# A new order of all engines for a one-core kernel of block attention and a gated MLP: fillers on TensorE, some VN on ScalarE, moved tiles

## The chip, the cores and the metric

One NeuronCore of a Trainium2 chip runs the whole program. The metric is the time of one execution on the device in microseconds (us). The engines are TensorE (PE; its weight loads are listed as PEld), VectorE (DVE), ScalarE (ACT), GpSimd (POOL) and SyncE (SP), which here only issues DMAs.

## What is computed

Inputs: q, k, v of 4 batches x 8 heads x 768 positions x 64, a decay lam per head, and the weights of a gated MLP. First comes linear attention with decay in blocks of 64, then the MLP with a mixing of positions:

```
for b in range(nb):                                    # blocks of 64 positions
    intra = (qb @ kb.T) * Dmask ; intra = intra @ vb   # inside the block
    inter = (qb * lam_pow) @ kv_state
    out[:, :, sl] = intra + inter
    kv_state = lam_block * kv_state + (kb * rev_pow).T @ vb
h = maximum(x @ w_in, 0)                               # x: heads side by side, 4 x 768 x 512
u, v = h[..., :512], h[..., 512:]
v_n = (v - mean(v)) / sqrt(var(v) + 1e-06)             # over the 512
v_s = einsum('ts,bsd->btd', w_spatial, v_n) + b_spatial[None, :, None]
out = (u * v_s) @ w_out                                # 4 x 768 x 512, float32
```

## The kernel before

The 4 x 768 positions are worked through in 12 steps n of 256 positions, three to a batch. The decay is folded into k and q by powers of lam counted from the middle of the sequence, so that scores need only a 0/1 mask and the state is only added to. All order is written out by hand: ORDER (from L16) is a list of tokens, each naming a step, its indices and, last, the engine (T TensorE, D VectorE, A ScalarE, P GpSimd, S SyncE). Each engine executes its tokens strictly in the order of the list; semaphores between engines follow from the tiles that are read and written. The last numbers of a token on TensorE and of the copies behind it are PSUM banks; bank 7 holds the running state.

The steps, by token:

- LK, LQ, LV load k, q, v of step n (512 KB each) into one of three buffers each; SP issues them, and the load of n waits until the buffer's last reader (KM or QM or QC, VC of n-3) is done.
- WI, WS, WO load the weights through GpSimd's queue with a cast to bf16, BS the bias through SP.
- LB, LN, LL, LX: powers of lam (Ln, a product, Exp). LT (L221) makes a second table of powers for q along the free dimension, from positions made by pos (L201).
- KM and QM (L287, both print as L289): k or q times its power, cast to bf16, half a step per token (kc, qc; two buffers each). QC (L282): q cast without the power. VC: v cast to bf16 (vb).
- TK and TQ: transposes of kc and qc on TensorE into PSUM; EK and EQ bring them to kT and qT, EQ (L332) multiplied by LT's table. From step 5 on DK and DQ do the transposes by DMA from SP instead, straight to kT and qT.
- SC: scores, MK (L354): mask and cast. KV: state update, SS: copy of the state. AV: attention output, in an inter part (L388) and an intra part (L397). FN: one-element copy that releases it. EX: copy to xT.
- PV (L422), PU (L460): x times the v and u half of w_in; EV and EU apply the relu.
- BN, RA, RD: mean and variance, square root, reciprocal. VN (L449 to L452): normalised v, on VectorE.
- WT, EW: transposes of w_spatial. GP puts the bias into PSUM, PW (L486) multiplies by w_spatial over all six 128-row tiles of a batch, GM multiplies by u. So PW of a batch needs every VN of that batch.
- PO (L497), EO, ST: product with w_out, copy, store. PH, EH, SH do one tile of the last batch in two halves.
- GT (L242): a one-element copy on GpSimd that holds a weight load back until an input has landed. `one` fills a tile of ones; FL (L265) would run matmuls on it whose result nobody reads, but no FL token is in this list.

In the old list PW of batch 0 begins after attention of steps 0 to 2 and the PV and PU of these; attention of step 3 comes between its PW tokens.

Of the kernel before, what the change touches and what calls it, by code (L numbers as in the profile page):

```python
# [16 lines left out]
one.D lam.A LK.0.S msk.P mkc.D LB.0.T LN.0.A posk.P LL.D LX.A KM.0.0.D pos.P idn.P TK.0.0.1.T KM.0.1.P  # L17
TK.0.1.2.T LQ.0.S QC.0.1.D TQ.0.1.3.T LT.0.A QC.0.0.P TQ.0.0.4.T EQ.0.0.4.D LT.1.A EQ.0.1.3.D LK.1.S KM.1.1.P
TK.1.1.5.T EK.0.0.1.A SC.0.0.3.4.T EK.0.1.2.A LQ.1.S QC.1.0.P EK.1.1.5.A GT.1.1.P WI.0.P KM.1.0.D LV.0.S
SC.0.1.0.1.T LV.1.S TK.1.0.6.T EK.1.0.6.A TQ.1.0.2.T LQ.2.S LK.2.S QC.1.1.P TQ.1.1.5.T MK.0.0.3.4.D EQ.1.0.2.D  # L20
MK.0.1.0.1.D VC.0.A KV.0.0.T AV.0.0.3.6.T SS.0.0.A FN.0.3.6.A LV.2.S QC.2.1.P BS.S LK.3.S GT.1.2.P WI.1.P
EQ.1.1.5.D SC.1.1.0.1.T SC.1.0.4.5.T MK.1.0.4.5.D KV.0.1.T SS.0.1.A KM.2.0.P GT.2.1.P WS.0.P LQ.3.S LT.2.A
AV.0.1.3.6.T LV.3.S LK.4.S VC.1.D KV.1.0.T LQ.4.S SS.1.0.A KV.1.1.T KM.2.1.P LK.5.S MK.1.1.0.1.D AV.1.0.2.4.T
QC.2.0.A TQ.2.1.5.T EX.0.1.6.D WS.1.P TQ.2.0.0.T EQ.2.0.0.D LQ.5.S VC.2.P FN.1.2.4.A AV.1.1.2.4.T LV.4.S
EX.1.0.2.D EQ.2.1.5.D EX.1.1.4.A PV.1.0.1.T EX.0.0.3.D SS.1.1.D PV.0.1.6.T EV.0.1.6.A PV.1.1.0.T EV.1.1.0.A
KM.3.0.P KM.3.1.P QC.3.2.P GT.2.2.P WO.P EV.1.0.1.D BN.1.0.D BN.0.1.D TK.2.0.2.T BN.1.1.D PV.0.0.5.T VC.3.P
TK.2.1.4.T EK.2.1.4.D EK.2.0.2.A SC.2.0.0.1.T MK.2.0.0.1.D SC.2.1.3.4.T MK.2.1.3.4.D EV.0.0.5.A RA.1.A BN.0.0.D
RA.0.A RD.1.D LV.5.S RD.0.D PU.1.0.6.T PU.1.1.2.T KV.2.0.T SS.2.0.A EU.1.0.6.A AV.2.0.0.1.T FN.2.0.1.D VN.0.0.D
VN.0.1.D PU.0.1.3.T EU.0.1.3.A KM.4.0.P AV.2.1.0.1.T EX.2.0.0.A EX.2.1.1.D GP.0.0.0.4.A EU.1.1.2.A GP.0.0.1.5.A
PU.0.0.6.T VN.1.1.D VN.1.0.D EU.0.0.6.D PV.2.0.3.T KM.4.1.P EV.2.0.3.A BN.2.0.D PV.2.1.0.T EV.2.1.0.A BN.2.1.D  # L30
WT.0.0.1.T WT.1.0.2.T EW.1.0.2.A EW.0.0.1.D RA.2.A RD.2.D VN.2.0.D WT.2.0.6.T EW.2.0.6.D PU.2.0.3.T GP.0.2.0.0.A
PU.2.1.2.T VN.2.1.D PW.0.0.0.4.T EU.2.0.3.A EU.2.1.2.A WT.1.1.1.T EW.1.1.1.A WT.2.1.6.T EW.2.1.6.A GP.0.3.0.3.D
GM.0.0.0.4.D GP.0.1.1.2.A PW.0.2.0.0.T GM.0.2.0.0.D GP.0.1.0.4.A WT.0.1.1.T EW.0.1.1.D PW.0.3.0.3.T TK.3.2.6.T
EK.3.2.6.A TQ.3.2.0.T PW.0.1.0.4.T GM.0.1.0.4.D EQ.3.2.0.D PW.0.1.1.2.T GM.0.1.1.2.D GM.0.3.0.3.D PW.0.0.1.5.T
GM.0.0.1.5.D KV.3.0.T SC.3.0.0.1.T MK.3.0.0.1.D SC.3.1.2.3.T MK.3.1.2.3.D GP.0.2.1.4.A PW.0.2.1.4.T TK.4.2.6.T
QC.4.2.A TQ.4.2.5.T EQ.4.2.5.D GM.0.2.1.4.D GP.0.3.1.0.A PW.0.3.1.0.T AV.3.0.1.2.T FN.3.1.2.D SS.3.0.A KV.3.1.T
KM.5.1.P EK.4.2.6.A SC.4.0.3.4.T GM.0.3.1.0.D KM.5.0.D DK.5.S AV.3.1.1.2.T EX.3.1.2.A EX.3.0.1.A SC.4.1.5.6.T
MK.4.1.5.6.D PO.0.2.0.T EO.0.2.0.A PO.0.4.2.T EO.0.4.2.D QM.5.1.P QM.5.0.D DQ.5.S VC.5.P PO.0.3.1.T PU.3.0.5.T
PV.3.1.6.T PV.3.0.0.T VC.4.A SS.3.1.D KV.4.0.T MK.4.0.3.4.D AV.4.0.2.3.T EV.3.0.0.D BN.3.0.D PO.0.5.4.T
EU.3.0.5.A SS.4.0.A KV.4.1.T EV.3.1.6.A BN.3.1.D LK.6.S KM.6.0.P FN.4.2.3.A AV.4.1.2.3.T EX.4.1.3.D SS.4.1.A  # L40
LV.6.S EX.4.0.2.A RA.3.A RD.3.D PO.0.1.0.T EO.0.1.0.A EO.0.3.1.A KV.5.0.T SC.5.0.5.6.T MK.5.0.5.6.D SC.5.1.2.3.T
MK.5.1.2.3.D SS.5.0.A PO.0.0.0.T EO.0.0.0.A LQ.6.S QM.6.0.P PV.4.1.1.T PV.4.0.5.T LK.7.S KM.7.0.P LQ.7.S
KM.6.1.D VN.3.0.D LQ.8.S DK.6.S EO.0.5.4.A AV.5.0.2.6.T FN.5.2.6.D PU.4.0.3.T EV.4.1.1.A EV.4.0.5.A QM.6.1.P
AV.5.1.2.6.T BN.4.0.D VC.6.A KV.6.0.T GP.1.2.0.0.D EX.5.0.2.D PU.4.1.4.T EU.4.0.3.A EX.5.1.6.A EU.4.1.4.A
VN.3.1.D BN.4.1.D PV.5.1.1.T EV.5.1.1.D RA.4.A RD.4.D BN.5.1.D PV.5.0.5.T LV.7.S EV.5.0.5.A BN.5.0.D RA.5.A
VN.4.1.D VN.4.0.D RD.5.D VN.5.0.D PU.3.1.2.T EU.3.1.2.A DQ.6.S QM.8.1.P QM.8.0.P VN.5.1.D KM.7.1.D DK.7.S
PU.5.0.3.T PU.5.1.6.T QM.7.1.D QM.7.0.D DQ.7.S PW.1.2.0.0.T EU.5.0.3.D SS.6.0.A GM.1.2.0.0.D LK.8.S LK.9.S
LV.8.S GP.1.3.1.4.A PW.1.3.1.4.T GP.1.0.0.1.A EU.5.1.6.A PW.1.0.0.1.T GM.1.3.1.4.D GM.1.0.0.1.D GP.1.0.1.5.A
PW.1.0.1.5.T GM.1.0.1.5.D GP.1.1.1.2.A PW.1.1.1.2.T SC.6.0.3.4.T MK.6.0.3.4.D SC.6.1.0.1.T MK.6.1.0.1.D
GP.1.2.1.6.A VC.7.A GP.1.3.0.5.A KV.6.1.T PW.1.3.0.5.T GM.1.3.0.5.D KM.8.1.P KM.8.0.P PW.1.2.1.6.T GP.1.1.0.3.A  # L50
SS.6.1.A PW.1.1.0.3.T GM.1.1.1.2.D GM.1.2.1.6.D AV.6.0.0.4.T FN.6.0.4.D KV.7.0.T SS.7.0.A SC.7.1.1.2.T
GM.1.1.0.3.D AV.6.1.0.4.T EX.6.1.4.A DQ.8.S SC.7.0.5.6.T DK.8.S KV.7.1.T PO.1.4.3.T EX.6.0.0.D PU.6.0.4.T
# [33 lines left out]
def kernel(  # L86
# [84 lines left out]
    def bank(b):  # L171
        return ps[:, b]
# [387 lines left out]
```

## Time and profile before

| | us |
|---|---|
| median of 3 runs | 153.12 (152.53 to 153.46) |
| span of the profiled execution, first to last instruction | 151.8 |
| TensorE busy in it | 133.6 |
| VectorE busy | 115.3 |
| ScalarE busy | 82.2 |
| GpSimd busy | 46.7 |

The profile is of one execution; its own time is given as its span of 151.8 us. Busy time is the time in which an engine had at least one instruction under way; a matmul's duration contains the latency of its pipeline, so matmuls overlap and a rate is read from the start-to-start distance in the chain, not from the mean duration. The chain of work that ended last is followed back from the last instruction and shows, at each moment, the work that the end waited for. DMA shares are of 16 engines and can exceed 1, where packets of several queues overlap.

### The profile page before, as it was taken

Reading aid. Unit: us, or ns where it says so; the run is one execution under the profiler, and the core shown is the slowest. Engines: PE = TensorE matmul, PEld = TensorE weight load, DVE = VectorE, ACT = ScalarE, POOL = GpSimd, SP = SyncE. Lnnn points to the kernel's source line nnn. Section 1 sums busy time; section 2 is a strip of 40 time slices with the busy share of each in tenths; the row PEclk is TensorE's granted clock in tenths of the full one; section 3 lists DMA queues with packets and bytes.
Section 4 is the critical chain, followed back from the end, with each engine's and each line's share of the span. In section 5 each row is a group of like instructions: output and inputs, shape, how many; then the busy total and the mean of one; then the engine's idle time right before and its main releaser. Section 6 shows DMA issues by size and latency. Waiting matters only on the chain.

```text
span 151.8 us, 4599 instructions
## 1 busy us (share of the span) xinstructions
PE 133.6 (88%) x1933; PEld 86.7 (57%) x1946; DVE 115.3 (76%) x216; ACT 82.2 (54%) x165; POOL 46.7 (31%) x59
## 2 busy tenths in 40 slices
PE   0287679998499999999999999999999999999990
PEld 0167553575367675556666757557566474666540
DVE  4466937799963799889998997779687888797620
ACT  3885710757247546389393447977622436842041
POOL 7594922059300008022504340275282000000000
PEclk9999999999969999999999999999999999999998
DMA  3999999999995003499998999998999978200424
GB/s 98 346 347 335 243 261 221 216 319 283 206 295 168 0 4 69 93 313 316 251 245 120 318 187 279 341 171 249 334 196 264 217 297 309 111 4 0 187 110 187
DMA packets 58375, 32.28 MB, mean 213 GB/s; under 512 B 15858, under 2 KB 55282, under 8 KB 58354
## 3 DMA queue, kind: packets, MB, share of 16 engines
q1 hardware_dynamic: 55968, 29.23, 73.9%
q0 software_dynamic: 2384, 2.75, 10.6%
q8 instruction: 15, 0.25, 0.6%
q14 instruction: 6, 0.05, 0.1%
q10 hardware_dynamic: 2, 0.00, 0.0%
HBM read 24.77 MB, written 6.29 MB: 205 GB/s over the span
## 4 chain that ended last, share of the span: by engine, by line
PE 74%; DVE 8%; ACT 2%; DMA 1%; issue 1%
PE ps L486 21%; PE ps L422 13%; PE ps L460 13%; PE ps L497 11%; PE ps L397 4%; DVE vn L451 4%; PE ps L367 3%; PE ps L350 3%; PE ps L388 2%; PE ps L319 2%; DVE a_sb L355 1%; DMA out_dram<-o_sb 1%; PE ps L472 1%; DVE xT L178 1%; DVE st L437 1%
## 5 line engine op out<-in xcount | busy, mean ns | idle before, releaser
L486 PE MATMUL ps<-wt_sb,vn 128*128 128x384 bf16 x192 | 33.5, 328 | 0.0
L289 POOL TENSOR_TENSOR kc<-k_in,lv 128x512 bf16<-128x512 f32 x18 | 19.1, 1071 | 41.4 <-PE ps L367 25.7
L355 DVE TENSOR_TENSOR a_sb<-ps,m 128x1024 bf16<-128x1024 f32 x24 | 28.6, 1214 | 2.8 <-PE ps L350 2.6
L422 PE MATMUL ps<-win_sb,xT 128*128 128x512 bf16 x92 | 25.0, 407 | 1.8 <-DVE xT L178 1.4
L486 PEld LDWEIGHTS <-vn 128*128 128x128 bf16 x192 | 18.5, 99 | 11.8 <-issue 0.3
L460 PE MATMUL ps<-xT,win_sb 128*128 128x256 bf16 x192 | 24.9, 283 | 0.0
L497 PE MATMUL ps<-wout_sb,gT 128*128 128x512 bf16 x83 | 21.7, 380 | 0.7 <-issue 0.3
L492 DVE TENSOR_TENSOR gT<-ps,uT 128x384 bf16<-128x384 f32 x32 | 16.6, 549 | 7.5 <-PE ps L486 6.6
L460 PEld LDWEIGHTS <-win_sb 128*128 128x128 bf16 x192 | 18.7, 101 | 4.5
L437 DVE BATCH_NORM_STATS2 st<-vh 128x6 f32<-128x512 bf16 x24 | 16.5, 686 | 3.8 <-ACT vh L427 3.6
L289 POOL TENSOR_TENSOR qc<-q_in,lqn 128x512 bf16<-128x512 f32 x11 | 11.9, 1089 | 19.8 <-DMA q_in<-in_q_dram 10.4
L176 ACT ACTIVATE ps<-bsp 128x384 f32<-128x384 f32 x26 | 12.5, 493 | 9.6 <-DVE gT L492 6.4
L427 ACT ACTIVATE vh<-ps 128x512 bf16<-128x512 f32 x19 | 11.3, 595 | 11.0 <-PE ps L422 11.0
L422 PEld LDWEIGHTS <-xT 128*128 128x128 bf16 x96 | 9.6, 104 | 12.9 <-issue 2.8
L176 ACT ACTIVATE o_sb<-ps 128x512 f32<-128x512 f32 x18 | 10.5, 596 | 11.5 <-PE ps L497 8.9
L451 DVE TENSOR_SCALAR vn<-vh,mv,rstd 128x512 bf16<-128x512 bf16 x24 | 13.7, 601 | 0.2
L497 PEld LDWEIGHTS <-gT 128*128 128x128 bf16 x92 | 8.3, 98 | 9.1
L176 ACT ACTIVATE xT<-ps 128x512 bf16<-128x512 f32 x15 | 8.5, 595 | 8.1 <-PE ps L397 8.1
L397 PE MATMUL ps<-a_sb,vb 64*64 64x128 bf16 x384 | 11.9, 233 | 0.3 <-issue 0.3
L427 ACT ACTIVATE uT<-ps 128x512 bf16<-128x512 f32 x17 | 9.9, 588 | 2.5 <-PE ps L460 2.5
L176 ACT ACTIVATE s_sb<-ps 128x256 bf16<-128x256 f32 x17 | 6.5, 380 | 8.8 <-PE ps L367 8.8
L367 PE MATMUL ps<-vb,kc 64*64 64x64 bf16 x320 | 9.3, 202 | 2.1 <-DVE vb L178 0.9
(70 smaller groups left out, 161.7 us busy)
## 6 DMA issues: line engine op xcount, KB each, us to landing
k_in<-in_k_dram SPq DMA_DIRECT2D x12, 512.0 KB, 5.6
q_in<-in_q_dram SPq DMA_DIRECT2D x12, 512.0 KB, 6.1
v_in<-in_v_dram SPq DMA_DIRECT2D x12, 512.0 KB, 7.2
out_dram<-o_sb SPq DMA_DIRECT2D x23, 256.0 KB, 4.1
wsp_raw<-in_moe_w_spatial_dram POOLq DMA_DIRECT2D x2, 576.0 KB, 12.4
win_sb<-in_moe_w_in_dram POOLq DMA_DIRECT2D x2, 512.0 KB, 9.4
wout_sb<-in_moe_w_out_dram POOLq DMA_DIRECT2D x1, 512.0 KB, 9.2
bsp<-in_moe_b_spatial_dram SPq DMA_DIRECT2D x1, 384.0 KB, 12.5
```

Of the source, the lines that this page charges most:

```text
L176: nc.scalar.activation(out=o, in_=i, func=AF.Copy)
L289: vec(e).tensor_tensor(out=dst[n % NCA][:, u].rearrange("p u m o d -> p o (u m) d"), in0=src[n % NIN].rearrange("p (o u) m d -> p o u m d" ...
L355: nc.vector.tensor_tensor(out=a_sb[n % NA][:, i].rearrange("p o w j x -> p o w (j x)"), in0=ps[:, b0:b1 + 1:b1 - b0].rearrange("p o (w y) ...
L397: nc.tensor.matmul(out=po[c ^ o][row(w), c, i], lhsT=vb[n % NCA][row(c), 4 * o + u, j, :], rhs=a[row(c), i, o, w, j, :], start=(r == 0 and ...
L422: nc.tensor.matmul(out=bank(b), lhsT=x[:, slot(c, g)], rhs=win_sb[:, g, DH:DFF], start=(g == 0), stop=(g == NCH - 1))
L427: nc.scalar.activation(out=o, in_=i, func=AF.Relu)
L437: nc.vector.bn_stats(out=st6[p2][:, t], in_=vh[p2][:, t])
L451: vec(e).tensor_scalar(out=vn[p2][:, t], in0=vh[p2][:, t], scalar1=mv[p2][:, t, 0:1], scalar2=rstd[p2][:, t:t + 1], op0=ALU.subtract, op1= ...
L460: nc.tensor.matmul(out=pu[:, f2].rearrange("p (c x) -> p c x", c=2), lhsT=win_sb[:, g, f * P:(f + 1) * P], rhs=x[:, slot(0, g):slot(1, g) ...
L486: nc.tensor.matmul(out=bank(b)[:, 0:HW], lhsT=vn[bb % 2][:, s, f * P:(f + 1) * P], rhs=wt_sb[:, s, i * HW:(i + 1) * HW], start=False, stop ...
L492: nc.vector.tensor_tensor(out=gT[bb % 2][:, f, cols], in0=bank(b)[:, 0:HW], in1=uT[bb % 2][:, f, cols], op=ALU.mult)
L497: nc.tensor.matmul(out=bank(b), lhsT=gT[bb % 2][:, f, t * P:(t + 1) * P], rhs=wout_sb[:, f, :], start=(f == 0), stop=(f == NCH - 1))
```

## The change

ORDER is replaced by another list of 671 tokens. What differs between the lists, apart from the sequence:

- Seven FL tokens on TensorE: 11, 108 and 23 matmuls of 128 columns, 2, 3 and 1 of 512, 1 of 256, all ahead of the first PV. They write to PSUM that is free at the time, or to unused columns of bank 7.
- q is always multiplied by its power in QM (24 tokens; 15 on GpSimd, 9 on VectorE). LT, pos, QC and GT are gone. EQ becomes a plain copy, 5 on VectorE and 5 on ScalarE.
- TK and TQ take half a step each (10 and 10) for steps 0 to 4; DK and DQ from step 5 as before.
- VN: 14 on VectorE, 10 on ScalarE (as Identity with scale and bias; RD then also computes the bias, one small VectorE operation for six of the steps).
- KM: 14 on GpSimd and 10 on VectorE (18 and 6 before). VC: 3 on ScalarE, 3 on VectorE, 6 on GpSimd (6, 2, 4). SS: 12 on ScalarE, 8 on VectorE (17, 3). GP: 22 and 10 (26, 6). EK: 4 and 6 (7, 1). EX: 17 and 7 (15, 9).
- PH, EH and SH become one more PO, EO and ST.
- Ln and Exp use one activation table, loaded at the start; the table for the square root is loaded by a token SQ of its own.
- Tiles are declared in another order: the small ones that are read by many instructions first, the rest of the small ones at the end, with the tables that are gone left out, so that starts fall on multiples of 256 bytes.
- The weight loads stand behind QM.2.1 (WI.0, WI.1), QM.6.0 (WS.0), KM.7.0 (WS.1) and VC.10 (WO) on GpSimd.

In the new list attention, PV and PU of steps 3 to 6 come ahead of the first PW of batch 0, and the first PW of batch 1 comes after attention of step 8. SP's new sequence:

```
LQ.0 LK.1 LK.0 LV.0 LQ.1 LV.1 LQ.2 LK.2 LQ.3 LK.3 LV.2 LV.3 LQ.6 LK.4 LQ.4 LV.4 LV.5 LQ.5 LK.5 LK.6 LK.7
DQ.5 DK.5 DK.6 DQ.6 LV.6 LQ.7 DK.7 DQ.7 LK.8 BS LV.7 LQ.8 LQ.9 LV.8 LV.9 LK.9 DQ.9 DK.8 DQ.8 LK.10 DK.9
LQ.10 LV.10 DK.10 LQ.11 DQ.10 LK.11 DK.11 DQ.11 LV.11 and then 24 ST
```

The core of the diff, with the first lines of the two lists:

```diff
-one.D lam.A LK.0.S msk.P mkc.D LB.0.T LN.0.A posk.P LL.D LX.A KM.0.0.D pos.P idn.P TK.0.0.1.T KM.0.1.P
-TK.0.1.2.T LQ.0.S QC.0.1.D TQ.0.1.3.T LT.0.A QC.0.0.P TQ.0.0.4.T EQ.0.0.4.D LT.1.A EQ.0.1.3.D LK.1.S KM.1.1.P
...
+one.D msk.P LQ.0.S LK.1.S lam.A FL.11.128.6.1.T LK.0.S posk.P LV.0.S idn.P LQ.1.S LB.0.T FL.108.128.6.1.T LV.1.S
+LN.0.A LL.D LQ.2.S LY.A LX.A LK.2.S KM.1.0.P QM.0.0.P KM.0.0.D KM.0.1.D VC.0.A QM.0.1.D KM.1.1.D LQ.3.S KV.0.0.T
+LK.3.S TK.0.1.1.T QM.1.1.P TK.1.1.2.T LV.2.S TQ.0.1.3.T EK.1.1.2.D FL.23.128.6.1.T EQ.0.1.3.A LV.3.S SS.0.0.D QM.1.0.P
+mkc.D EK.0.1.1.D SC.0.1.4.5.T TK.0.0.6.T MK.0.1.4.5.D TQ.1.1.0.T EK.0.0.6.A KV.0.1.T TQ.0.0.2.T SS.0.1.A
+FL.2.512.1.1.T EQ.1.1.0.D EQ.0.0.2.A QM.2.0.P VC.1.A SC.0.0.3.4.T SC.1.1.5.6.T QM.2.1.P MK.0.0.3.4.D FL.3.512.2.1.T
+WI.0.P TQ.2.1.1.T KM.2.1.D AV.0.0.0.2.T TQ.2.0.3.T MK.1.1.5.6.D WI.1.P FN.0.0.2.A AV.0.1.0.2.T TQ.1.0.4.T QM.3.1.P
+FL.1.256.7.0.T EX.0.0.0.D EQ.1.0.4.A TK.1.0.5.T KV.1.0.T EK.1.0.5.A EQ.2.1.1.D KM.2.0.P SS.1.0.A SC.1.0.0.1.T
+EX.0.1.2.A KV.1.1.T MK.1.0.0.1.D VC.2.P EQ.2.0.3.A TK.2.1.6.T TK.2.0.4.T KM.3.0.P EK.2.0.4.D AV.1.0.5.2.T EK.2.1.6.D
+FL.1.512.3.1.T KM.3.1.D SC.2.0.0.1.T FN.1.5.2.D SS.1.1.D AV.1.1.5.2.T MK.2.0.0.1.D SC.2.1.3.4.T EX.1.1.2.A TK.3.1.6.T
+KV.2.0.T EX.1.0.5.A QM.3.0.D TK.3.0.2.T SS.2.0.A PV.0.1.0.T VC.3.A EK.3.1.6.D LQ.6.S MK.2.1.3.4.D PV.0.0.1.T LK.4.S
...
     def c_lam(e):
         nc.scalar.dma_start(out=lam_in, in_=lam.unsqueeze(0))
+        nc.scalar.preload_act_table_set("natural_log_exp_and_others")
...
     def l_x(e):
-        nc.scalar.activation(out=lqn, in_=lv, func=AF.Exp, scale=-1.0)
-        nc.scalar.activation(out=lv, in_=lv, func=AF.Exp)
+        nc.scalar.activation(out=lv, in_=lraw, func=AF.Exp)
+
+    def l_y(e):
+        nc.scalar.activation(out=lqn, in_=lraw, func=AF.Exp, scale=-1.0)
+
+    def t_sq(e):
+        nc.scalar.preload_act_table(AF.Sqrt)
...
     def f_l(e, k, w, b, new):
+        cols = slice(T2, T2 + w) if b == SB else slice(0, w)
         for i in range(k):
-            nc.tensor.matmul(out=bank(b)[:, 0:w], lhsT=ones[:, 0:P], rhs=ones[:, 0:w],
+            nc.tensor.matmul(out=bank(b)[:, cols], lhsT=ones[:, 0:P], rhs=ones[:, 0:w],
                              start=(new == 1 and i == 0), stop=True, skip_group_check=True)
...
     def e_q(e, n, x, b):
-        nc.vector.tensor_tensor(out=qT[n % NTR][:, part(x)].rearrange("p u m x -> p (u m x)"),
-                                in0=quad(b)[:, part(x)].rearrange("p u m x -> p (u m x)"),
-                                in1=lq[:, n % NR, part(x)].rearrange("p u m x -> p (u m x)"), op=ALU.mult)
+        copy(e, qT[n % NTR][:, part(x)].rearrange("p u m x -> p (u m x)"),
+             quad(b)[:, part(x)].rearrange("p u m x -> p (u m x)"))
...
     def r_d(e, n):
...
+        nc.vector.reciprocal(out=rstd[p2][:, cols], in_=rstd[p2][:, cols])
+        if f"VN.{n}.0.A" in TOKENS or f"VN.{n}.1.A" in TOKENS:
+            nc.vector.scalar_tensor_tensor(out=nmr[p2][:, cols], in0=mv[p2][:, cols, 0], scalar=-1.0,
+                                           in1=rstd[p2][:, cols], op0=ALU.mult, op1=ALU.mult)
...
     def v_n(e, n, c):
         t, p2 = 2 * (n % NR) + c, n // NR % 2
+        if e == "A":
+            nc.scalar.activation(out=vn[p2][:, t], in_=vh[p2][:, t], func=AF.Identity,
+                                 scale=rstd[p2][:, t:t + 1], bias=nmr[p2][:, t:t + 1])
+            return
```

## The prediction

> **What bounds the kernel now.** I read the page's shares first, then the windows of 5 us, then the chain, then the instructions of the stretch in which TensorE idles, then the DMA queues.
>
> ```profile
> PE 133.6 (88%) x1933; PEld 86.7 (57%) x1946; DVE 115.3 (76%) x216; ACT 82.2 (54%) x165; POOL 46.7 (31%) x59
> PEclk9999999999969999999999999999999999999998
> ```
> 88% is an average over two different stages. The windows (columns: PE, PEld, DVE, ACT, POOL, clock, DMA share, GB/s) separate them:
> ```profile
> 5.00:10.00 5.00, 2.47 (x20) 1.88 (x20) 2.47 (x4) 4.96 (x13) 3.76 (x4) 1.00 1.15 347
> 20.00:25.00 5.00, 3.95 (x40) 2.27 (x39) 2.79 (x6) 0.76 (x2) 1.03 (x1) 1.00 1.16 232
> 35.00:40.00 5.00, 2.60 (x20) 1.34 (x20) 5.00 (x5) 3.07 (x6) 4.26 (x6) 1.00 0.93 248
> 40.00:45.00 5.00, 4.60 (x28) 3.16 (x28) 4.09 (x11) 1.79 (x4) 0.00 (x0) 0.66 1.15 254
> 50.00:55.00 5.00, 5.00 (x85) 3.44 (x84) 4.83 (x8) 2.50 (x5) 0.00 (x0) 1.00 0.00 0
> 105.00:110.00 5.00, 5.00 (x35) 3.13 (x33) 3.71 (x9) 3.79 (x7) 0.76 (x1) 1.00 1.15 341
> ```
> From 44 us on TensorE never rests; before that it idles or runs slow. DMA rests at 50 us. The chain (start, us, what):
> ```profile
> 23.49 4.28 PE ps L422 x10
> ...
> 36.04 3.71 DVE vn L451 x2
> ...
> 40.89 3.13 PE ps L460 x16
> 44.02 1.26 PE ps L486 x6
> ...
> 90.74 0.86 PE ps L422 x4
> ...
> 102.98 2.62 PE ps L460 x24
> 105.60 4.87 PE ps L486 x30
> ```
> The same L422 matmul steps at 428 ns at 23 us and 215 ns at 90 us, so TensorE ran at half rate at 23 us although the clock row still prints a 9; L460 at 40.9 us is slow likewise (196 against 109 ns, and there the row shows 0.66). VN (L451), normally 0.41 us, holds the chain for 3.71 us; the instructions show GpSimd beside it:
> ```profile
> 35.97 3.78 DVE L451 TENSOR_SCALAR vn<-vh,mv,rstd 128x512 bf16<-128x512 bf16 x2
> 36.22 1.05 POOL L180 CAST vb<-v_in 128x1024 bf16<-128x1024 f32 x1
> 37.22 2.04 POOL L289 TENSOR_TENSOR kc<-k_in,lv 128x512 bf16<-128x512 f32 x2
> ```
> ```profile
> q1 hardware_dynamic: 55968, 29.23, 73.9%
> q0 software_dynamic: 2384, 2.75, 10.6%
> ```
>
> **TensorE's own work.** Full-rate prices from the chain's steady part: PW 0.974 us (4.87/5), PV and PO 0.862, PU 0.872, SC 0.23, KV 0.25, AV 0.46 (0.24 inter, 0.22 intra), a 128-wide transpose 0.0556 (0.89/16), WT 0.34. With 32, 24+24, 24, 24, 20, 24, 80 and 6 of them (and less for the four AV without an inter part) that is 120.9 us in both kernels; the two PH become one PO, which is nothing. Before PW.0.0.0 starts at 44.02 us only 19.6 us of it are done, and the other 101.3 us end at 148.03: 104.0 us, a factor of 1.027. So about 24 us can be gained at the start, and nearly nothing after it. The span of 151.8 leaves 3.8 us behind the last PO (copy, store). The median 153.12 is 1.4 us over the span; I add that to my span.
>
> **Part 1: fillers and the earlier start.** The 142 narrow, one 256-wide and six 512-wide fillers cost 142 x 0.0556 + 0.11 + 6 x 0.215 = 9.3 us at full rate. All stand ahead of the first PV, where TensorE waits for loads and VectorE, so I cost them at nothing; without that cover they cost 9.3. They should make the 12 first PV and the PU behind them run at 215 and 109 ns: 12 x 0.21 = 2.6 us at 23 to 27 us. The half-rate stretch at 40.5 to 43.9 us has to go by part 3. The trace has no filler; the bounds are 0 (TensorE still drops to half rate in a gap) and 2.6 us, and I take 2.6 since the steady part shows a full clock wherever TensorE is fed. The Trainium skill, "TensorE: Matmul & The Clock Gate", Part 1, puts the release after about 3.4 us of sustained activity; by that the fillers suffice. Its Part 4 (PE-mode transpose) says that transposes do not count as such activity, which would speak against the stretch from 12 to 25 us, thin in matmuls; by it the first 2.6 us would be lost again.
>
> **Part 2: when the first PV can start.** Landings before come at 4.8, 6.2, 7.7 and 9.3 us: one 512 KB load per 1.5 us. In the new SP order q0 k1 k0 v0 q1 v1 q2 k2 land at 4.8 to 15.3. VC.0 (1.05 us on ACT) makes v0 ready at 10.4. DVE: KM.0.0, KM.0.1, QM.0.1, KM.1.1 from k0 at 7.8, 4 x 0.69 = 2.8, so 10.6; then the transposes of TensorE (to about 12), EK 0.4, SS 0.4, mkc 1.2, EK 0.4: 14.4; SC.0.1 follows and MK.0.1 starts near 14.9. From there to PV.0.1.0 VectorE has five MK at 1.16 (2.36 for two), two KM and one QM at 0.62, two EQ and two EK at 0.32, EX 0.61, SS 0.35, FN: 10.0 us, so 24.9. POOL: QM.1.1 waits for q1 (10.8), QM.2.0 for the transposes that read qc (about 15.6), so WI.0 is issued at 17.7. WI.0 took 9.5 us from issue to landing before: 27.2. From below: issue 0.85, 2.5 (the first load's 4.0 less its 1.5) and 2.7 of transfer, 23.7. I take 25.5 for the first PV. The merged Ln/Exp table saves one 1.28 us load on ACT; LX ends a microsecond earlier, hidden behind k0. The dropped LT, pos, QC and GT (LT 5.0 us of ACT, pos 1.6 and QC 3.7 us of POOL) lie beside this and are counted as 0; QM takes their place.
> At 25.5 us 17.0 - 9.3 = 7.7 us of real work are done, as much as before at that time. The gain must come from what follows.
>
> **Part 3: the rest, 113.2 us.** PW.0 now waits until 33 us more of TensorE work has been placed ahead of it (attention, PV, PU of blocks 3 to 6), so the VN and statistics of batch 0 are off the path. If TensorE stays fed: 113.2 x 1.027 = 116.2, end at 141.7, against 148.03.
> Is it fed? VectorE: from the first PV to PW.2.0.0 TensorE has 80.3 us and VectorE, by start-to-start intervals in its full rows (MK 1.16, BN 0.80, GM 0.49, VN 0.35, EX 0.61, KM and QM 0.62, GP 0.47), 79.1. Ten VN move to ACT (0.60 each; ACT ends at about 75 to 82 us in all, covered), but 10 more KM/QM, 5 SS and 4 GP come to VectorE. GpSimd's blocking cost VectorE before about 4.0 us on VN (13.7 - 24 x 0.405), 0.7 on KM, 0.6 on QC: 5.3 in 34 SBUF-only operations; after there are 36. Bounds 0 and 5.7; at 3 VectorE needs 82.1 of TensorE's 82.4. No gap by itself, no slack either. The Trainium skill, "SBUF — State Buffer", Who interferes with whom, says of this shared port pair that the loser "fully blocks", also a VectorE operation with two SBUF inputs against a GpSimd read; the row above agrees (3.78 us for two), and by it the 19 KM and QM on VectorE are as exposed as the VN were.
> DMA: SC.11.0 stands at 81.4 us of TensorE's list, 64.4 behind the first PV: wanted at 25.5 + 66.1 = 91.6 us. Before it happens at 121.5. Before it must land 35 loads x 1.5 = 52.7, bsp 1.1, the weights 14.0 (10.6% of 151.8 us over the share of 1.15 seen at full load) and 14 transposes. These: 73.9% is 112.2; less 25.5 MB at 347 GB/s (73.6 x 1.15 = 84.7) leaves 27.5, so 2.0 each or 1.7 us at 1.15; at 1.36 (the highest window) less, about 1.2. Sum with 3.3 us before the flow: 88 to 95 us, if DMA never rests. SP is moved heavily: LQ.6 stands ahead of LK.4 and waits for QM.3 (about 24 us), but the queue then still has WI and v3 to move (to 27 us); DQ.5 and DK.5 wait for k5 and POOL, in time for SC.5 at 46 to 48. I take 2.5 us of lateness in all, between 0 and 3.3 (95 - 91.6) and near the upper end, because SP's waits leave some rest.
>
> **Other edits.** Tile addresses: no row shows an effect; MK at 1.16 and loads at 347 GB/s bound it, I take 0. SQ moves the third table load (1.28 us, ACT) to where ACT has room. ST: 24 stores, all late, 24 x 0.76 = 18 us in the last 45 us; the tail has the same form, 3.8.
>
> **Sum.** 91.6 + 2.5 + 48.8 x 1.027 (50.1) + 3.8 = 148.0 span, 149.4 us.
>
> **Rivals.**
> (a) TensorE-bound throughout: WI.0 lands by 23.7 and DMA is never late: 23.7 + 116.2 + 3.8 + 1.4 = 145.1. For it: before kept TensorE full with VectorE at 4.8 of 5. Against: VectorE without slack. Chance 0.22.
> (b) Slower: transfers become the bound. With the DMA resting 5% of the time, SC.11.0 starts at 3.3 + 91.6/0.95 = 99.7, not 91.6, and the end is 99.7 + 50.1 + 5.2 = 155.0; at 11% rest, as in before from 62 to 118 us, 161.5. It decides from 97.8 us (153.1 - 55.3) on. For it: the list now wants block 11 thirty microseconds earlier. Against: before had a DMA rest of some 17 us (45 to 65) that is now filled. 0.20 beyond 154.7.
> (c) The changes cancel: VectorE's blocking stays at 5.7 and the fillers do not hold the clock (2.7 + 2.6): 154.7; or half of it, 152. With the milder part of (b) 0.18 for within 1%.
> Forecast (147 to 151.5): 0.40.
>
> **Numbers.** A measurement tells about 1% (151.6 to 154.7). Faster 0.62, same 0.18, slower 0.20. The range leaves out a tenth at each end: 144 to 157.
>
> **What would show it.** Right: L422 at about 215 ns from its first use near 25.5 us, no half-rate window at 40 us, VN near 0.41 us, TensorE at 5.0 of 5 from about 26 us, SC.11 near 94 us, last PO ending 3.8 us before the span. Wrong: PE idle before SC or TK with a DMA as releaser (b), PE idle behind MK or EX with VectorE at 5.0 (blocking), first PV beyond 28 us (WI late), or a clock of 0.5 after 12 us.

## The result, and the profile after

The changed kernel takes 171.08 us (median of 5 runs, 168.87 to 174.58) against 153.12 (5 runs, 152.53 to 153.91): it is slower, ratio 1.111 [1.104, 1.118]. Medians here are over all runs of a kernel, ratios over its fast ones alone, those within 1.5% of its fastest. Its profiled execution has a span of 168.3 us, against 151.8 before. The forecast was 149.4 us, range 144 to 157: wrong, and on the other side.

The shares and the clock row of the changed kernel's page, and its DMA queues:

```profile
PE 142.7 (85%) x2091; PEld 93.2 (55%) x2091; DVE 114.8 (68%) x224; ACT 76.2 (45%) x156; POOL 43.3 (26%) x50
PEclk9999999999999999699999999999999999999999
q1 hardware_dynamic: 55824, 29.23, 65.7%
q0 software_dynamic: 2384, 2.75, 9.6%
```

The same bytes move as before, in a longer span. The windows of the changed kernel (same columns as those of before):

```profile
5.00:10.00 5.00, 5.00 (x86) 5.00 (x84) 2.18 (x3) 0.76 (x1) 2.04 (x2) 1.00 1.15 347
40.00:45.00 5.00, 5.00 (x76) 3.07 (x73) 4.91 (x9) 2.07 (x4) 3.88 (x4) 1.00 1.16 295
60.00:65.00 5.00, 4.04 (x58) 2.24 (x49) 3.85 (x10) 4.72 (x10) 2.09 (x2) 1.00 0.60 70
105.00:110.00 5.00, 3.94 (x50) 2.09 (x48) 4.25 (x8) 1.61 (x3) 1.49 (x1) 1.00 0.25 56
```

At 40 us the new order does what was expected of it: TensorE 5.00 of 5, full clock, DMA at 1.16. At 60 and 105 us both rest for a part of the same 5 us: TensorE for about 1 us each, DMA at a share of 0.60 and 0.25. That points to a chain, in which each waits for the other.

What TensorE waited for, by its matmul instructions (start, duration, instruction, in brackets the idle time before it and its releaser), the waits over 0.9 us behind the opening:

```profile
30.38 0.44 PE L349 MATMUL ps<-vb,kc 64*64 64x64 bf16 x16 [2.57 <-ACT vb L173]
57.80 0.44 PE L349 MATMUL ps<-vb,kc 64*64 64x64 bf16 x16 [1.62 <-POOL vb L177]
67.11 1.07 PE L332 MATMUL ps<-qT,kT 64*64 64x128 bf16 x32 [3.00 <-DMA qT<-qc]
72.69 2.17 PE L476 MATMUL ps<-wt_sb,vn 128*128 128x384 bf16 x12 [1.14 <-ACT ps L173]
86.88 0.93 PE L332 MATMUL ps<-qT,kT 64*64 64x128 bf16 x32 [1.05 <-DMA qT<-qc]
92.40 0.42 PE L332 MATMUL ps<-qT,kT 64*64 64x128 bf16 x16 [2.63 <-DMA kT<-kc]
100.13 0.42 PE L332 MATMUL ps<-qT,kT 64*64 64x128 bf16 x16 [1.21 <-DMA qT<-qc]
116.04 0.44 PE L349 MATMUL ps<-vb,kc 64*64 64x64 bf16 x16 [2.61 <-POOL vb L177]
```

L332 is SC and waits for the transposed copies of k and q; L349 is KV and waits for VC, which had waited for a v load. All but one belong to the supply of the attention steps. The other one, PW at 72.69, waits for the bias that ScalarE copies into PSUM (GP), and that copy for the bias load (BS), issued at 66.15 behind k8 and landed 5.9 us later; so it hangs on SP's queue too. In the kernel before, TensorE has no wait over 0.9 us at all behind 44 us. The DMA-issuing instructions of SP between 38 and 68 us (the third column SPq) show how the supply is chained:

```profile
38.08 1.38 SPq L188 DMA_DIRECT2D k_in<-in_k_dram  x1
45.62 1.34 SPq L289 DMA_TRANSPOSE qT<-qc  x1
47.05 2.65 SPq L285 DMA_TRANSPOSE kT<-kc  x2
49.80 2.16 SPq L289 DMA_TRANSPOSE qT<-qc  x1
52.02 0.57 SPq L188 DMA_DIRECT2D v_in<-in_v_dram  x1
52.65 0.57 SPq L188 DMA_DIRECT2D q_in<-in_q_dram  x1
54.00 4.35 SPq L285 DMA_TRANSPOSE kT<-kc  x1
64.24 1.23 SPq L289 DMA_TRANSPOSE qT<-qc  x1
65.52 0.58 SPq L188 DMA_DIRECT2D k_in<-in_k_dram  x1
```

Here q7 (issued at 52.65) stands behind the copies of steps 5 and 6, though its buffer was free at 38.3; it lands at 62, QM.7 runs, DQ.7 goes out at 64.24, SC.7 starts at 67.1; and k8 (65.52) stands behind DQ.7, though its buffer was free at 44.1.

The first rows of SC.5 and SC.11, before (L350):

```profile
65.97 0.24 PE L350 MATMUL ps<-qT,kT 64*64 64x128 bf16 x2
121.29 0.62 PE L350 MATMUL ps<-qT,kT 64*64 64x128 bf16 x32
```
and after (L332):
```profile
50.44 0.42 PE L332 MATMUL ps<-qT,kT 64*64 64x128 bf16 x16
112.48 0.62 PE L332 MATMUL ps<-qT,kT 64*64 64x128 bf16 x32
```

| us | before | forecast | after |
|---|---|---|---|
| first PV | 22.7 | 25.5 | 25.9 |
| SC.5 | 66.0 | 46 to 48 | 50.4 |
| SC.11 | 121.3 | 94 | 112.5 |
| from SC.5 to SC.11 | 55.3 | 46 to 48 | 62.0 |
| TensorE work listed in between | 53.7 | 44.4 | 44.4 |
| end of the span | 151.8 | 148.0 | 168.3 |

The fifth row is counted from the two orders with the forecast's prices. Before, six attention steps took 55.3 us with 53.7 us of TensorE work laid between them. The new order lays 44.4 us between them, and they take 62.0.

### The profile page after: what moved, and what is told of

It is laid out like the page before. It is cut to its first block, busy times and chain, and to the rows that moved or that the text cites. A ratio compares the mean times of both kernels' runs of the same rounds, so it can differ in the third digit from the quotient of the medians.

```text
span 168.3 us, 4889 instructions
## 1 busy us (share of the span) xinstructions
PE 142.7 (85%) x2091; PEld 93.2 (55%) x2091; DVE 114.8 (68%) x224; ACT 76.2 (45%) x156; POOL 43.3 (26%) x50
## 4 chain that ended last, share of the span: by engine, by line
PE 42%; DMA 26%; SPq 10%; DVE 8%; issue 6%; ACT 2%; POOL 2%; POOLq 1%; DVEq 0%; ACTq 0%
DMA v_in<-in_v_dram 14%; PE ps L487 12%; PE ps L476 9%; SPq L188 6%; PE ps L450 6%; PE ps L255 5%; DMA k_in<-in_k_dram 4%; PE ps L404 4%; DMA q_in<-in_q_dram 3%; DMA qT<-qc 3%; DMA kT<-kc 2%; SPq L289 2%; PE ps L349 2%; POOL kc L272 2%; DVE a_sb L337 1%
## 5 line engine op out<-in xcount | busy, mean ns | idle before, releaser
L272 POOL TENSOR_TENSOR kc<-k_in,lv 128x512 bf16<-128x512 f32 x14 | 14.9, 1073 | 37.4 <-DMA k_in<-in_k_dram 20.6
L404 PE MATMUL ps<-win_sb,xT 128*128 128x512 bf16 x96 | 23.9, 384 | 0.0
L487 PE MATMUL ps<-wout_sb,gT 128*128 128x512 bf16 x96 | 22.9, 379 | 0.0
L450 PEld LDWEIGHTS <-win_sb 128*128 128x128 bf16 x192 | 18.5, 100 | 4.8 <-issue 0.2
L272 POOL TENSOR_TENSOR qc<-q_in,lqn 128x512 bf16<-128x512 f32 x15 | 16.0, 1078 | 18.8 <-DMA q_in<-in_q_dram 10.2
L409 ACT ACTIVATE vh<-ps 128x512 bf16<-128x512 f32 x21 | 12.2, 591 | 17.7 <-PE ps L404 14.3
L332 PE MATMUL ps<-qT,kT 64*64 64x128 bf16 x384 | 10.5, 227 | 9.9 <-DMA qT<-qc 5.5
L332 PEld LDWEIGHTS <-kT 64*64 64x64 bf16 x384 | 7.4, 111 | 12.7 <-issue 6.5
L349 PE MATMUL ps<-vb,kc 64*64 64x64 bf16 x320 | 8.6, 194 | 6.8 <-POOL vb L177 4.2
L173 ACT ACTIVATE ps<-bsp 128x384 f32<-128x384 f32 x22 | 10.5, 489 | 7.2 <-DVE wt_sb L175 7.2
L255 PE MATMUL ps<-ones 128*128 128x128 bf16 (+2 forms) x149 | 12.1, 246 | 1.6 <-DVE ones L250 1.6
L272 DVE TENSOR_TENSOR kc<-k_in,lv 128x512 bf16<-128x512 f32 x10 | 7.8, 788 | 7.5 <-DMA k_in<-in_k_dram 7.5
```

The source lines that it names most:

```text
L173: nc.scalar.activation(out=o, in_=i, func=AF.Copy)
L255: nc.tensor.matmul(out=bank(b)[:, cols], lhsT=ones[:, 0:P], rhs=ones[:, 0:w], start=(new == 1 and i == 0), stop=True, skip_group_check=True)
L272: vec(e).tensor_tensor(out=dst[n % NCA][:, u].rearrange("p u m o d -> p o (u m) d"), in0=src[n % NIN].rearrange("p (o u) m d -> p o u m d" ...
L332: nc.tensor.matmul(out=pa[o][row(c), w, j], lhsT=kT[n % NTR][row(o), u, j, c * Q64:(c + 1) * Q64], rhs=qv(n, o, u, c), start=(w == 0 and j ...
L404: nc.tensor.matmul(out=bank(b), lhsT=x[:, slot(c, g)], rhs=win_sb[:, g, DH:DFF], start=(g == 0), stop=(g == NCH - 1))
L409: nc.scalar.activation(out=o, in_=i, func=AF.Relu)
```

## The experiments

The kernels ran beside the kernel before on the same chip (its medians there: 153.2 to 153.6). The runs of one changed kernel spread by 1.5 to 8 us, so differences of about 2 us between two such medians say nothing. "After" is the changed kernel, "the middle" the stretch from SC.5 to SC.11. The profiled execution took longer than its kernel's median in four cases (readiness order, 170.75; quarter copies, 169.54; three buffers without fillers, 174.39; 119 fillers, 164.69), so the middles of these are rather too long. Where an order takes more lines, the line numbers behind it move by 1 to 5.

**SP in order of readiness.** Only SP's tokens of steps 4 to 11 change place:
```diff
-LQ.6 LK.4 LQ.4 LV.4 LV.5 LQ.5 LK.5 LK.6 LK.7 DQ.5 DK.5 DK.6 DQ.6 LV.6 LQ.7 DK.7 DQ.7 LK.8 BS LV.7 ...
+LK.4 LQ.4 LV.4 LV.5 LQ.5 LK.5 LQ.6 LK.6 LK.7 LV.6 LQ.7 DK.5 DQ.5 LV.7 DK.6 DQ.6 LK.8 LQ.8 DK.7 LV.8 DQ.7 ...
```


> The changed kernel with only SyncE's tokens in another order: loads whose buffer is long free no longer stand behind DMA transposes that wait for KM and QM. Theory A (SP's queue is blocked: 112.5 us at SC.11.0 comes from transfers that could have been made earlier): SC.11.0 near 100 us, time near 158 us. Theory B (the volume due before SC.11 is the bound, any order is as late): SC.11.0 stays beyond 108 us, time 167 to 171 us.

Measured: 168.43 (165.84 to 170.75), middle 61.7. The loads do come earlier (q7 issued at 41.7 for 52.7), but the profiled execution gains nothing in the middle, and SC.5 comes later (54.3 for 50.4). Two things stand against the gain in its trace: copies now stand behind loads in the transfers, and GpSimd's QM.7, ready sooner, meets KM.7.1 on VectorE, 3.33 us for 0.69. What the first is worth was not tested; the second is tested below.

**Copies with a quarter of their bytes.** The scores of steps 5 to 11 then use stale data for three quarters:
```diff
-nc.sync.dma_start_transpose(kT[n % NTR].rearrange("p u m x -> p (u m) x"), ...
+nc.sync.dma_start_transpose(kT[n % NTR].rearrange("p u m x -> p (u m) x")[:, 3:5], ...
```


> The changed kernel with DMA transposes of a quarter of the bytes (the middle quarter of kc and qc, which waits for the same KM and QM); the other three quarters of kT and qT keep old contents. Order and waits are the same, 14 x 0.75 x 1.7 = 18 us of transfers are gone. Theory A (blocked queue): about 165 us, since the loads still wait behind the same transposes. Theory B (volume): SC.11.0 near 96 us and 154 to 157 us.

Measured: 167.14 (two runs, 164.75 and 169.54), middle 59.9. Its clock ran at half rate from 66.6 to 76.8 us, 6.8 us longer than in the changed kernel (shown below), which by an estimate costs 3.4 us, half of that. So the bytes of the copies are worth 2 to 5.5 us of the middle and are not the whole loss.

**No copies.** All DK and DQ tokens are left out; the scores of steps 5 to 11 use old tiles.

> The changed kernel without any DMA transpose (kT and qT keep the contents of steps 3 and 4). SP then waits for nothing but free buffers. Theories A and B: first PV at 26 us as before, TensorE nearly full from there, 146 to 152 us. Rival C (VectorE and the blocking by GpSimd hold the middle stage): stays above 160 us.

Measured: 155.25, middle 50.1. No TensorE wait for a transfer over 0.9 us is left behind 28 us; the longest is for VectorE, where GpSimd again blocks KM.7.1 (3.15 us at 52.9):
```profile
57.23 0.50 PE L332 MATMUL ps<-qT,kT 64*64 64x128 bf16 x16 [2.01 <-DVE a_sb L337]
```
So the copies carry 16 us, but this run takes away their wait, their bytes, their place in SP's queue and the buffers they hold, all at once.

**No fillers.** All FL tokens are left out.

> The changed kernel without the 149 filler matmuls. If the fillers buy the full clock in the opening but the transfers bind later (A or B): the first PV comes 1 to 3 us later with matmuls at half rate, the end moves by 0 to +3 us (170 to 174 us). If the fillers themselves delay real work: 162 to 168 us.

Measured: 163.96, ratio to before 1.058 [1.047, 1.068]: 7 us faster than after, with a first PV 3 us later (28.8). SC.4 starts at 40.4 (after: 40.7): the lead of the early clock is gone by then. The middle takes 54.6.

**Three buffers for kc, qc, vb, kT, qT**, order kept:
```diff
-NIN, NCA, NTR, NA, NX, NO = 3, 2, 2, 2, 3, 12
+NIN, NCA, NTR, NA, NX, NO = 3, 3, 3, 2, 3, 12
```


> The changed kernel with three buffers in place of two for each of kc, qc, vb, kT and qT; the order of every engine is kept. It asks for the loop: KM.n must wait for KV.(n-2), the transposed copy of step n for KM.n, and SC.n for that copy, some 5 us after KM.n. With a third buffer KM.n waits for KV.(n-3). If this loop is what holds the middle (theory D), SC.7 comes by 63, SC.11 by 106 in place of 112.5 us and the time is 160 to 165. If SP's queue alone holds it (theory A), no load is issued sooner, since LQ.7 and LK.8 stand behind the same copies: SC.11 within 2 us of 112.5 and 169 to 173.

Measured: 172.28. KM.7.0 does start 2.9 us sooner (48.2). But the weights WS.1 stand right behind it on GpSimd and go out sooner too (49.2 for 52.1), and SC.5 comes 4.1 us later (54.5), q7 is issued 5.4 us later (58.0). The middle itself is shorter, 58.6 for 62.0. So the buffer count alone does not give the time back, but this run does not clear it: it moved the weights as well.

**Readiness order and no fillers together**, then **with three buffers too**:

> The changed kernel without its 149 filler matmuls and with SP's loads and copies in the order in which their buffers and sources are ready (the two edits tried one at a time before: 163.96 and 168.43 us). If the two losses are separate they add up: 171.1 - 7.1 - 2.6 = 161.4. If the fillers only made the same queue later, the second edit finds little left: 163 to 166.

> As the one before, with three buffers for kc, qc, vb, kT and qT too. Theory D (the loop through two buffers) with A: SC.11 by 100, as without any transposed copies, and a time of 153 to 157. If the buffers' count plays no part: the time of the one before, within 1.5 us, and what is left in the middle is the order on VectorE, GpSimd and TensorE.

Measured: 166.98 and 173.78 (167.60 to 174.43). They don't add up. In the second, GpSimd, free to run earlier, holds VectorE's VC.5 for 5.23 us; the instructions of the two engines:
```profile
41.62 5.23 DVE L175 CAST vb<-v_in 128x1024 bf16<-128x1024 f32 x1
42.26 1.05 POOL L272 TENSOR_TENSOR kc<-k_in,lv 128x512 bf16<-128x512 f32 x1
43.26 1.05 POOL L272 TENSOR_TENSOR qc<-q_in,lqn 128x512 bf16<-128x512 f32 x1
44.26 2.03 POOL L272 TENSOR_TENSOR kc<-k_in,lv 128x512 bf16<-128x512 f32 x2
```
The CAST ends at 46.85, 0.56 us after the last of GpSimd's multiplications. The Trainium skill, "SBUF — State Buffer", Who interferes with whom, calls the port pair that VectorE and GpSimd share an exclusive lock whose loser "fully blocks", and counts casts among the operations that can take it. The trace agrees, 5.23 us for the usual 0.69, and shows more: the CAST, begun at 41.62 while GpSimd issued weights, stays blocked through the four GpSimd instructions that follow.

**Readiness order and small copies together** (scores as in the second run):

> The changed kernel with both edits that gave little alone: SP's loads and copies in the order of readiness (168.43 alone) and the transposed copies cut to a quarter of their bytes, so that its scores are of part of the data only (167.14 alone). If each took away one of two holds of the same chain (loads behind waiting copies; copies behind loads in the same transfers), both together come near the kernel without transposed copies: 155 to 160. If the loss lies in neither, 165 to 167.

Measured: 164.37, middle 54.5. The two do add up, but more than half of what leaving the copies out gives is still missing (9 of 16 us).

**The blocked half of KM.7 on GpSimd**, on the kernel with readiness order and no fillers:
```diff
-KM.7.0.P ... KM.7.1.D
+KM.7.0.P KM.7.1.P ...
```


> The changed kernel without fillers and with SP's order by readiness (166.98), and with the second half of KM.7 moved from VectorE, where it took 3.3 us in place of 0.7 while GpSimd multiplied q7, to GpSimd ahead of q7. If the blocking of VectorE is what ate the gain of the earlier loads, some 3 us come back and more where the copies of step 7 start sooner: 160.5 to 164.5. If the chain of copies holds it anyway: 166 to 168.

Measured: 166.94, as without it. The block is gone from the trace; DK.7 is issued 1 us sooner but takes 4.9 us to issue behind loads, and SC.7 starts at 68.9 (68.6).

**The spatial weights earlier**: WS.1 moved ahead of KM.6.0 on GpSimd, issued at 44.9 in place of 52.1 us.

> The changed kernel with one token moved: GpSimd issues the second half of the spatial weights (576 KB) ahead of KM.6.0, at 44 us, where the transfers rest, in place of 52.1, just ahead of q7's load at 52.7. Without fillers the two came the other way round (q7 at 53.7, weights at 54.5) and q7 landed 6.0 in place of 9.4 us after its issue. If this race is what the fillers cost: SC.7 by 64.5 in place of 67.1 and 164 to 168. If the loss with fillers comes from something else: 169.5 to 172.5.

Measured: 170.76. SC.7 comes later (69.6), not sooner. The weights now run ahead of DQ.5 and DK.5; SP's issues and TensorE's wait in this kernel:
```profile
45.85 1.51 SPq L290 DMA_TRANSPOSE qT<-qc  x1
47.46 6.31 SPq L286 DMA_TRANSPOSE kT<-kc  x2
56.49 0.64 PE L333 MATMUL ps<-qT,kT 64*64 64x128 bf16 x16 [5.88 <-DMA kT<-kc]
```
Two kT copies take 6.31 us to issue (after: 2.65), and SC.5 starts at 56.5 (50.4). With 576 KB ahead of the copies that are waited for, SC.5 came 6 us later here; by SC.11 the time has come back (110.3 for 112.5). The Trainium skill, "DMA: Bandwidth & Descriptors", Issuing engines are not separate DMA queues, says that DMAs of all issuing engines run on the same 16 DMA engines and interleave; this row agrees, GpSimd's weights hold SP's copies.

**The first 119 fillers only** (FL.11 and FL.108, in the wait for the first k and v; the 30 among the work left out):

> The changed kernel with only the first 119 fillers, those in the wait for the first k and v; the 30 among the work from 11.7 to 23 us are left out. If the lead that the early clock gives is what hurts later (loads and copies meeting in another order): 168 to 172, as with all of them. If the 30 are what costs: 163 to 166, as with none.

Measured: 163.11, ratio to before 1.054 [1.050, 1.057]. Its four runs took 161.25, 161.53, 164.69 and 169.61. So the 119 cost nothing, and gain nothing that these medians show (163.96 without any), while the 30 cost 8 us by the medians, three times the 2.7 us that they last. How they cost it is not shown. The first PV comes no later with them (25.9, and 26.2 without), nor do the scores and the first weights ahead of it. What comes later is v3. It is issued at 16.7 us in both, just ahead of the first weights, and lands 12.5 us after that with the 30 and about 7.2 without, so VC.3 runs at 25.90 in place of 29.27 us, the 2.57 us wait at KV.3 is gone and SC.4 starts at 38.7 (40.7). But without any fillers VC.3 runs at 28.96 and SC.4 at 40.4, and that kernel is as fast, so the late v3 does not explain it alone. From SC.5 on, reached within 0.3 us of each other (50.7), both kernels issue the same instructions, and this one needs 57.3 us for the middle in place of 62.0.

**The parts for the opening, in the old order.** 145 fillers of 128 columns ahead of the first PV; VN.0 and VN.1 on ScalarE; both:

> The kernel before with 145 filler matmuls of 128 columns put into TensorE's idle stretches ahead of the first PV (into unused columns of bank 7). Prediction's term: the clock is full from about 6 us on, and the 2.6 us that half rate costs until 26.9 are gone, if VectorE and the loads do not take them: 150 to 152.5. If fillers cost by themselves what leaving them out gave in the changed kernel (7 us): 157 to 161. If the opening waits for loads and VectorE: 152.5 to 154.5.

> The kernel before, with the four normalizations VN.0 and VN.1 on ScalarE in place of VectorE, the part of the change that speaks of the blocking. VectorE lost 4.4 us there to GpSimd between 33 and 40 us, and TensorE idles 2.3 us at 40 and 1.1 at 44. If the opening's bound is VectorE: 149.5 to 152. If the work there waits for the loads: 152.5 to 154.5.

> The kernel before with both parts that aim at its opening: 145 fillers of 128 columns ahead of the first PV and the four normalizations VN.0 and VN.1 on ScalarE. Alone they gave 153.2 and 152.1 beside 153.5 and 153.2. If the clock and VectorE each hide the other, both together give 148.5 to 151; if the opening waits for the loads in any case, 151.5 to 153.5.

Measured: 153.2, 152.11 and 152.52. Alone, neither can be told from the kernel before; both together give a ratio of 0.995 [0.991, 0.999]. Their profiles show what was meant: a mean clock of 0.997 and more, the four VN at 0.8 us each on ScalarE, PW.0 at 41.1 to 42.6 in place of 43.8 us. Half a per cent is too little to count as faster, and two of the eight runs with both took 158.0 and 158.8. But 145 fillers cost the old order nothing: fillers do not cost by themselves what the 30 cost.

**Transposes of steps 5 to 11 by TensorE in place of the copies** (112 transposes, 28 moves by ScalarE and VectorE): with all fillers, with none, with 119 and both halves in one bank, and with 119 into banks that stay free longest. In the first three a bank that held a transpose is taken next by a bias write in two to five places, and their output is wrong; the fourth has no such place, and its output is right. So the gating's bias is probably lost there (argued, no trace shows it), and these three don't compute all, whatever their expectations say.

> The changed kernel, complete, with the transposed copies of steps 5 to 11 made by TensorE (112 transposes of 0.0556 = 6.2 us) and moved out by ScalarE and VectorE (28 of 0.4 us) at the places in the order where the copies were issued. If the wait for the copies (some 5 us from product to scores, seven times) is the loss: 155.3 without any, plus 6.2 us of transposes, less what of it fills idle time: 156 to 163. If their room in the order is the loss, and not the wait: 168 to 176.

> As the one before, without the 149 fillers. If the fillers cost by what they do to the transfers of the middle, which the copies share, the cost is gone with the copies: within 2 us of the one before. If they cost by themselves: 5 to 8 us less than the one before.

> The changed kernel, complete, with the first 119 fillers only (163.11 us with the copies) and the transposes of steps 5 to 11 made by TensorE, both halves of a step into one bank, moved out by ScalarE and VectorE. In the two runs before it (with the gating's bias partly lost) the time was 173 and the idle time of TensorE behind 26 us stayed at 19 us, its waits now for VectorE. If that holds: 168 to 174, so VectorE and GpSimd are as near to being the bound of the middle as the copies are. If the split of the halves over two banks cost them: 158 to 164.

> The changed kernel, complete, with the first 119 fillers only (163.11 us with the copies), the transposes of steps 5 to 11 made by TensorE into banks that no other instruction wants for as long as can be, never one that a bias is written to next. The runs before lost some 9 us to the next user of the bank (14 times 0.65). If the wait for the copies holds the middle: 156 to 161, that is the 10 us of TensorE's waits for loads and copies less 6.2 us of transposes or more. If VectorE and the loads hold it as well: 163 to 170.

Measured: 173.09, 173.58, 176.41 and 171.81; the last one complete, its middle 63.0 us for 48.9 us of listed work. So with the copies gone and the computation kept nothing is won: beside the same 119 fillers with copies (163.11) it is 9 us slower. Two of its TensorE waits:
```profile
61.47 0.38 PE L307 MATMUL ps<-ident,kc 128*128 128x128 bf16 x4 [1.26 <-DVE a_sb L342]
90.52 0.43 PEld L307 LDWEIGHTS <-kc 128*128 128x128 bf16 x7 [0.70 <-issue]
```
TensorE now waits at L307 (TK, TQ), in many short pieces: the longest ends with a mask on VectorE, and over the whole run the weight loads there sit idle for 6.1 us in 11 pieces whose end the profile puts down to nothing. That leaving the copies out recovers 16 us therefore does not mean that the copies' wait alone is what costs.

## Why the prediction was wrong

**Part 2, the opening: right.** First PV 25.9 (25.5 forecast), KV.0.0 at 10.7 (v0 ready at 10.4), WI.0 issued at 17.5 (17.7).

**Part 1, clock and blocking: right in mechanism; the cost of nothing: wrong.** The first eight PV matmuls take 1.89 us (before, ten took 4.28), and VN on VectorE never exceeds 0.53 us (before: 3.46). An instruction row and the summary of the tile vn:
```profile
25.91 1.89 PE L404 MATMUL ps<-win_sb,xT 128*128 128x512 bf16 x8
```
```profile
L441 DVE TENSOR_SCALAR vn<-vh,mv,rstd x14: 380/407/530, 62.8 to 144.2; 128x512 bf16<-128x512 bf16 x14
```
"All stand ahead of the first PV, where TensorE waits for loads and VectorE, so I cost them at nothing" holds for 119 of them. The other 30 cost 8 us (163.11 against 171.08). The named cover held as far as the first PV, which came no later with them; what they cost shows only behind it, and how is open. It belongs to this order: in the readiness order leaving all fillers out changed the median by 1.5 us (168.43 to 166.98), with TensorE's transposes by nothing (173.09 to 173.58).

**Part 3, "I take 2.5 us of lateness in all": the step that failed.** SC.11 came at 112.5, 18.5 us behind the 94 forecast, and this alone turns the result round: the rest, from SC.11 on, took 55.8 us against 50.1 + 3.8, and 2.6 of that is the wait for v11. The volume was sized nearly rightly. From 3 us to SC.11 (DMA share is the number ahead of the last):
```profile
3.00:26.00 23.00, 20.66 (x462) 17.27 (x462) 15.36 (x26) 8.34 (x18) 11.83 (x12) 1.00 1.13 300
26.00:46.00 20.00, 17.20 (x335) 11.58 (x333) 16.08 (x27) 9.53 (x18) 8.39 (x9) 1.00 1.07 285
46.00:67.00 21.00, 16.10 (x318) 11.02 (x316) 15.84 (x33) 15.55 (x33) 5.85 (x6) 1.00 0.85 158
67.00:92.00 25.00, 20.17 (x262) 12.96 (x262) 17.16 (x35) 11.36 (x24) 8.14 (x8) 0.93 1.05 246
92.00:113.00 21.00, 18.33 (x356) 11.51 (x360) 16.43 (x29) 8.39 (x19) 5.92 (x6) 1.00 0.87 163
```
Share times length sums to 109.8, that is 95.5 us at the full share of 1.15. The forecast's 88 to 95 contains 3.3 us before the flow, so this is about 4 us over its upper end. It took 110 us, so the equivalent of 14.5 us was rest. The forecast summed the transfers over the whole time, as if they could run ahead. They can't: a load needs one of three input buffers, a copy needs a product, a product needs a load, and all loads and copies go out in one order. From SC.5 on the supply of the steps must be moved at the pace of the steps. By the forecast's own prices that is 3 x 1.5 + 2 x 1.7 = 7.9 us a step, 47.4 for six, against 44.4 us of TensorE work, with no rest and no latency counted. Before had 53.7 us of work there, which covered them. But the volume is not what held the middle, as these windows show, the first of the changed kernel and the second of the one with a quarter of the copies' bytes:
```profile
50.44:112.48 62.04, 49.69 (x838) 31.80 (x842) 44.97 (x84) 31.00 (x67) 18.96 (x18) 0.97 0.94 194
```
```profile
50.66:110.57 59.91, 51.22 (x839) 32.37 (x842) 45.53 (x83) 30.68 (x67) 18.96 (x18) 0.91 0.66 164
```
At the full share of 1.15 the first moved 50.7 us of transfers and the second 34.4, well under the 44.4 us of work, and yet the second took 59.9, of which its half rate explains about 5. What the forecast put at 2.5 us is, as far as the runs show, the waiting along the chain from load to product to copy to scores: of the waits listed above, 10.7 us lie in the middle.

What holds the flow below its full rate is not one link. SP's queue, the copies' bytes, the third buffer, the blocking and the weights' place each moved the median by less than 4 us when changed alone (the blocking on the readiness order without fillers), with both signs; the third buffer cost 6.8 us on top of the readiness order without fillers; the best two together gave 7. Of the edits to the supply only leaving the copies out wholly gave 16, and that leaves the scores of steps 5 to 11 without their data; with the transposes kept, on TensorE, nothing came back.

**Rival (b)** had the right sign and the right point of decision: SC.11 fell beyond 97.8, and its rule (SC.11 plus 55.3) gives 167.8 for the 171.1 measured. It was given 5 and 11% of rest; 13% was measured (14.5 of 110). With 7.9 us a step beside 7.4 us of work its chance of 0.20 was too small. That its rule came so near is in part luck: "transfers become the bound" does not fit the quarter copies, which moved far less and gained little.

**VectorE's room: not put to the test.** The 82 us were set beside 82 us of TensorE from the first PV to PW.2.0.0; that stretch took 105.5 us (25.9 to 131.4), with VectorE busy for some 80. Without the copies VectorE was busy for 46.4 of the middle's 50.1 us, so it was close to the bound there. **Tail: right**, TensorE full from 116.4 to 164.4, then 3.9 us.

**Left open:** why the same instructions from SC.5 on need 62.0 us with the 30 fillers and 57.3 without. The race between q7 and the weights was tried as the cause and was not it. What of the copies' 16 us is latency and what the buffers they hold was not separated, nor why transposes on TensorE in their place were no faster.

## What to carry to other kernels

Check the supply not only as a sum over the whole time but over each stretch that the buffers close off: when each load and copy can start and how long it takes to land, against the work that the order lays between two steps. The sum of bytes alone would not have told: with 34.4 us of transfers the stretch still took 59.9. An order that brings supplied work forward and pushes unsupplied work to the end leaves less work to cover these waits; here 44.4 us in place of 53.7. And cost fillers by measuring them where they stand: 119 in a pure wait cost nothing here, 30 among the work cost 8 us in this order, though the first PV came no later for them.

## What the runs showed of the hardware that had not been expected

A transposed copy took 1.2 us to issue on SP when the transfers rested (64.24 us in the changed kernel) and up to 5.7 us when loads or weights were queued ahead (51.67 us with three buffers); in that time SP issued nothing else. After the 3.00 us wait at SC.7 the clock ran at half rate from 67.2 to 70.6 us, 3.4 us; half of that, 1.7 us of work, is an estimate of what was lost. The Trainium skill, "TensorE: Matmul & The Clock Gate", HAM oscillation, describes such waits for transfers and puts the window at about 3.4 us; here a wait of 3.0 us was enough. Shorter ones were too in the kernel with 119 fillers, where half rate followed waits of 2.32 us (at 50.7) and 2.69 us (at 70.7), while the changed kernel kept its full clock after waits of 2.57, 2.63 and 2.61 us. So the length of the wait alone does not decide. Two kernels with the same opening list held the clock differently: 1.00 up to 26 us with 119 fillers and copies, 0.79 with 119 fillers and TensorE's transposes later on. The window of the first:
```profile
0.00:26.00 26.00, 19.88 (x441) 17.28 (x441) 15.32 (x28) 9.81 (x20) 14.35 (x22) 1.00 1.03 277
```
and that of the second:
```profile
0.00:26.00 26.00, 21.55 (x365) 18.92 (x369) 13.19 (x23) 8.54 (x16) 13.94 (x22) 0.79 0.98 267
```
